# Reordering the stretch between dz and the dx loop of a fused transformer-block backward kernel: both dz halves together, dWq blocks between dKV and WK2, x normalised early, ring transposes ahead of those of WV2

## The chip, the cores and the metric

The kernel runs on one core of one Trainium2 chip. The metric is the device time of one execution in microseconds (us). The span of a profiled execution, from its first instruction to its last, is some 2 us shorter than its own timed value; what lies in between is not in the record, so spans are compared with spans and times with times.

## The reference, cut to what matters

The forward pass is a linear-attention block behind a LayerNorm, then a SwiGLU block behind another; S = 2048, D = 640, 32 heads of 20. The kernel returns the output and six gradients.

```python
def _A_ref(x, wqkv, wo):
    q, k, v = ...                       # x @ wqkv, 32 heads
    pq, pk = phi(q), phi(k)             # elu-like feature map
    kv = einsum("bhsd,bhse->bhde", pk, v)
    z  = einsum("bhsd->bhd", pk)
    o  = einsum("bhqd,bhde->bhqe", pq, kv) / (einsum("bhqd,bhd->bhq", pq, z)[..., None] + 1e-6)
    return o @ wo
h  = x + _A_ref(_layernorm(x), wqkv, wo)
h2 = h + _B_ref(_layernorm(h), w_gate, w_up, w_down)   # SwiGLU
# returned: h2 and the gradients of x, wqkv, wo, w_gate, w_up, w_down
```

The stretch in question belongs to the backward pass of the attention block: `dz` is the gradient of z, `dKV` that of kv, `WK2` and `WV2` are two weight matrices folded from dKV (WV2 is WK2 transposed), `dWq` and `dWk` are column blocks of the gradient of wqkv, and the last loop makes `dk`, `dxn` and from it the gradient of x, tile by tile.

## The kernel before: the parts that matter

TensorE and ScalarE are ordered by the framework's scheduler here; VectorE and the queue of SyncE (SP), which issues all DMA transposes, keep the order of the program. There are four PSUM tiles, the memory that matmuls write to, shared by everything (`mm`): a group of matmuls can take a tile only after VectorE or ScalarE has read out (evicted; "cast" where ScalarE makes bf16 of it) what an earlier group left there. The `ring` holds ten transposed operands for the coming tiles of the dx loop; a tile t is 128 of the 2048 rows. `dz` uses the TensorE array as tiles of 32 columns, all other matmuls here use all 128 columns; going from one to the other is called a tiling switch below.

```python
        ps_dz = mm("ps_dz")
        def dz_half(ci):                      # 16 matmuls on 32-column tiles of the array
            n0, n1 = NCH[ci]
            for t in range(ST):
                q = t % 4 * H
                nc.tensor.matmul(ps_dz[q:q + H, ci, :320], lhsT=nS1[:, t, :], rhs=pqs_tm[:, t, n0:n1], ...)
        dz_half(0)
        kv_blocks(dKVT, "ps_dkvt", ...)       # 6 blocks of 5 matmuls, each evicted by VectorE
        dz_half(1)
        ...                                   # dzE, dzL on VectorE out of ps_dz
        for t in range(ST):                   # x normalised, 16 tiles on VectorE
            nc.vector.tensor_scalar(out=xn_r[:, t, :], in0=xn_r[:, t, :], ...)
        def wk2(i):                           # 7 small matmuls, cast on ScalarE, transpose into WV2
            ps = mm("ps_wk2")
            mm_heads(ps, lambda j: wqkvT[:, 10 + j, i * P:(i + 1) * P], lambda j, a, b: dKVT[:, j, a:b])
            nc.scalar.copy(out=half(WK2[:, i, :]), in_=row(ps))
            nc.sync.dma_start_transpose(out=WV2[:, :, i * P:(i + 1) * P], in_=WK2[:, i, :])
        for i in range(DT):
            wk2(i)
        ps = mm("ps_dzb")                     # dz summed and broadcast: 4 matmuls of dzE, dzL
        ...
        for v in range(3):
            load_pqT(v)                       # 2 transposes each into the ring: pk, dq of tile v
        dwqk(0, 0, 3)                         # dWq blocks 0 to 2: 32 matmuls each, of x and dq
        for t in range(ST + LAG):             # the dx loop, LAG = 3
            ...                               # dk of tile t, transposed into the ring (SP)
            if t < HG: tr_cols(G[:, t, :], scr_GT, OH[t])             # one more transpose a tile (SP)
            elif t < 2 * HG: tr_cols(Y[:, t - HG, :], scr_Yt, OH[t - HG])
            u = t - LAG
            ...                               # dxn of tile u: dqT, pkT with WV2, dkT; 30 matmuls
            load_pqT(u + 3)
```

## Time and profile before

| | us |
|---|---|
| time, median of the first 3 runs | 821.05 (821.0 to 822.56) |
| span of the profiled execution | 820.0 |
| first dz matmul to first dk matmul, TensorE | 19.17 |
| first dk to first dxn matmul | 14.13 |
| first dxn matmul to the end | 169.7 |

From the profile's page, the busy time of the engines (us, share of the span, instructions), then the busy tenths of TensorE and its granted clock in 40 slices:

```profile
PE 813.3 (99%) x5540; PEld 521.0 (64%) x5540; DVE 442.9 (54%) x874; ACT 290.9 (35%) x412; POOL 187.6 (23%) x345
...
PE   8999999999999999999999999999999999999998
...
PEclk9999999999999999999999999999999999999999
```

TensorE is busy from end to end at full clock. Holes in it are short, and most of them do not show as idle time in the views: matmuls overlap in the trace (one of 320 columns lasts 299 ns there, while the next can start 136 ns after it). A hole is therefore read as the difference of two starts less the pace. The lines of the timelines of the stretch are in the prediction below.

### The profile page before, as it was taken

Reading aid. Unit: us, or ns where it says so; the run is one execution under the profiler, and the core shown is the slowest. Engines: PE = TensorE matmul, PEld = TensorE weight load, DVE = VectorE, ACT = ScalarE, POOL = GpSimd, SP = SyncE. Lnnn points to the kernel's source line nnn. Section 1 sums busy time; section 2 is a strip of 40 time slices with the busy share of each in tenths; the row PEclk is TensorE's granted clock in tenths of the full one; section 3 lists DMA queues with packets and bytes.
Section 4 is the critical chain, followed back from the end, with each engine's and each line's share of the span. In section 5 each row is a group of like instructions: output and inputs, shape, how many; then the busy total and the mean of one; then the engine's idle time right before and its main releaser. Section 6 shows DMA issues by size and latency. Waiting matters only on the chain.

```text
span 820.0 us, 14053 instructions
## 1 busy us (share of the span) xinstructions
PE 813.3 (99%) x5540; PEld 521.0 (64%) x5540; DVE 442.9 (54%) x874; ACT 290.9 (35%) x412; POOL 187.6 (23%) x345
## 2 busy tenths in 40 slices
PE   8999999999999999999999999999999999999998
PEld 6776656555555555555566677777776777777675
DVE  6878776891087018810760147787884366631212
ACT  6982422770184126500741122322322133322010
POOL 3330022322412412221125311211210111112330
PEclk9999999999999999999999999999999999999999
DMA  9994589998769997894498757976498999899962
GB/s 297 186 343 113 140 174 281 307 204 176 191 126 209 203 224 160 185 245 115 106 237 171 256 139 217 222 205 166 116 216 171 170 167 187 167 198 272 222 176 76
DMA packets 278321, 158.61 MB, mean 193 GB/s; under 512 B 235052, under 2 KB 264877, under 8 KB 278256
## 3 DMA queue, kind: packets, MB, share of 16 engines
q1 hardware_dynamic: 251696, 82.12, 54.3%
q0 software_dynamic: 17744, 64.45, 25.8%
q10 hardware_dynamic: 8816, 11.16, 4.3%
q8 instruction: 43, 0.70, 0.4%
q14 instruction: 22, 0.18, 0.1%
HBM read 47.68 MB, written 53.66 MB: 124 GB/s over the span
## 4 chain that ended last, share of the span: by engine, by line
PE 82%; DVE 9%; ACT 3%; DMA 3%; issue 1%; SPq 1%; ACTq 0%; POOL 0%; DVEq 0%
PE ps_dw L627 21%; PE ps_dhn L109 14%; PE ps_dxn L877 8%; PE ps_o L937 7%; PE ps_dwqk L109 5%; PE pu L563 5%; PE pg L558 5%; PE ps_y L109 3%; PE ps_gt L678 3%; PE ps_dp L109 3%; PE ps_dk L109 3%; PE pdm L385 2%; DMA xr<-in_A_x_dram 2%; PE ps_dm L385 2%; DVE st L134 1%
## 5 line engine op out<-in xcount | busy, mean ns | idle before, releaser
L109 PE MATMUL ps_dhn<-wgT,cols 128*128 128x320 bf16 x864 | 119.5, 299 | 0.0
L627 PE MATMUL ps_dw<-dd,hn 128*128 128x448 bf16 (+1 forms) x640 | 118.8, 346 | 0.0
L109 PEld LDWEIGHTS <-cols 128*128 128x128 bf16 x864 | 84.5, 98 | 32.9
L627 PEld LDWEIGHTS <-hn 128*128 128x128 bf16 x640 | 62.6, 98 | 54.2
L629 DVE CAST dwev<-ps_dw 128x896 bf16<-128x896 f32 (+3 forms) x12 | 10.9, 907 | 122.9 <-PE ps_dw L627 122.9
L629 ACT CAST dwev<-ps_dw 128x896 bf16<-128x896 f32 (+1 forms) x20 | 17.6, 879 | 160.5 <-PE ps_dw L627 139.9
L592 POOL DMA_DIRECT2D scr_dT<-stg x64 | 34.7, 542 | 168.9 <-DMA stg<-dd 168.2
L147 DVE CUSTOM_DVE_ANT_0 lb_a<-lb_dy,hn 128x640 bf16<-128x640 bf16 x32 | 26.4, 825 | 75.4 <-ACT lb_dy L145 75.4
L563 PE MATMUL pu<-wgu,hnT 128*128 128x448 bf16 (+1 forms) x320 | 63.6, 346 | 0.0
L558 PE MATMUL pg<-wgu,hnT 128*128 128x448 bf16 (+1 forms) x320 | 63.6, 346 | 0.0
L937 PE MATMUL ps_o<-wd,mT 128*128 128x320 bf16 (+3 forms) x462 | 61.3, 295 | 0.0
L627 PE MATMUL ps_dw<-m_s,dh 128*128 128x448 bf16 (+1 forms) x320 | 60.5, 346 | 0.1
L877 PEld LDWEIGHTS <-ring 128*128 128x128 bf16 x480 | 47.0, 98 | 18.2
L937 PEld LDWEIGHTS <-mT 128*128 128x128 bf16 (+1 forms) x462 | 41.8, 97 | 17.6 <-issue 2.6
L877 PE MATMUL ps_dxn<-wqkvT,ring 128*128 128x320 bf16 x320 | 51.3, 299 | 0.0
L627 PEld LDWEIGHTS <-dh 128*128 128x128 bf16 x320 | 31.3, 98 | 27.4 <-issue 0.4
L563 PEld LDWEIGHTS <-hnT 128*128 128x128 bf16 x320 | 31.3, 98 | 27.1
L558 PEld LDWEIGHTS <-hnT 128*128 128x128 bf16 x320 | 31.3, 98 | 27.0
L298 PE MATMUL ps_kq<-wqk,xnT 128*128 128x320 bf16 x320 | 46.4, 299 | 1.0 <-ACT xnT L290 1.0
L385 PEld LDWEIGHTS <-dh2T 128*128 128x128 bf16 x320 | 31.1, 98 | 25.1 <-issue 0.2
L385 PE MATMUL ps_dm<-wdT,dh2T 128*128 128x448 bf16 (+1 forms) x240 | 46.9, 344 | 0.1
L145 ACT ACTIVATE lb_dy<-ps_dhn,rstd 128x640 bf16<-128x640 f32 x16 | 12.7, 793 | 85.5 <-PE ps_dhn L109 85.5
(162 smaller groups left out, 1277.1 us busy)
## 6 DMA issues: line engine op xcount, KB each, us to landing
scr_dT<-stg POOLq DMA_DIRECT2D x48, 224.0 KB, 3.3
cols<-scr_dT POOLq DMA_DIRECT2D x6, 1728.0 KB, 8.0
scr_m<-m_s POOLq DMA_DIRECT2D x12, 448.0 KB, 4.7
cols<-scr_dT ACTq DMA_DIRECT2D x2, 1728.0 KB, 9.5
out_dram<-dwev POOLq DMA_DIRECT2D x30, 112.0 KB, 3.4
scr_dT<-stg POOLq DMA_DIRECT2D x16, 192.0 KB, 2.6
scr_pk<-pk SPq DMA_DIRECT2D x4, 640.0 KB, 8.4
scr_pq<-pqa SPq DMA_DIRECT2D x4, 640.0 KB, 8.7
```

Source lines behind the costliest of these rows:

```text
L109: nc.tensor.matmul(ps[:, ci, :320], lhsT=lhs(k), rhs=rhs(k, *NCH[ci]), start=(start and k == 0), stop=(stop and k == n - 1))
L147: nc.vector.tensor_tensor_reduce(out=a[:], in0=dy[:], in1=xhat, scale=1.0, scalar=0.0, op0=ALU.mult, op1=ALU.add, accum_out=sums[:, 1:2])
L298: nc.tensor.matmul(ps[:, ci, :320], lhsT=xnT[:, t, k, :], rhs=wqk[:, k, w0 + n0:w0 + n1], start=(k == 0), stop=(k == DT - 1))
L385: nc.tensor.matmul(ps[:, c, :w], lhsT=dh2T[:, kt, (t + c) * P:(t + c + 1) * P], rhs=wdT[:, kt, o:o + w], start=(kt == 0), stop=(kt == DT - 1))
L558: nc.tensor.matmul(pg[:, c, :w], lhsT=hnT[:, kt, (t + c) * P:(t + c + 1) * P], rhs=wg[:, kt, 0:w], start=(kt == 0), stop=(kt == DT - 1))
L563: nc.tensor.matmul(pu[:, c, :w], lhsT=hnT[:, kt, (t + c) * P:(t + c + 1) * P], rhs=wg[:, kt, w:2 * w], start=(kt == 0), stop=(kt == DT - 1))
L592: nc.gpsimd.dma_start(out=scr_dT[t + c, :, KO[g]:KO[g] + GK[g], :], in_=stg[:, :GK[g], :])
L627: nc.tensor.matmul(ps[:, c, :w], lhsT=lhs(t), rhs=rhs(t), start=(t == 0), stop=(t == ST - 1))
L629: copy(out=ev[:, :len(parts), :w], in_=ps[:, :len(parts), :w])
L678: nc.tensor.matmul(ps[:, ci, :320], lhsT=dh1[:, t, i * P:(i + 1) * P], rhs=pqs_tm[:, t, n0:n1], start=(t == 0), stop=(t == ST - 1))
L877: nc.tensor.matmul(ps[:, ci, :320], lhsT=lhs[:, i, :], rhs=rhs[:, i, n0:n1], start=(k == 0 and i == 0), stop=(k == 2 and i == DT - 1))
L937: nc.tensor.matmul(po(t, ci), lhsT=mTs[t // 4][r, t % 4, j, :], rhs=wd[r, j, n0:n1], start=(t, ci) not in opened, stop=last)
```

## The change

The intent is to take the waits out of TensorE between dz and the dx loop. The same instructions run in another order: the dz halves stand together, the dWq blocks are spread between dKV and the WK2 blocks so that there is work while ScalarE casts, the 16 normalisations that dWq needs are moved to where VectorE idled, and the first six transposes of the dx loop go ahead of those of WV2, which now come later.

```diff
+        for v in range(3):
+            load_pqT(v)
+        for t in range(ST):                   # x normalised: moved up
+            nc.vector.tensor_scalar(out=xn_r[:, t, :], ...)
         ps_dz = mm("ps_dz")
-        dz_half(0)
-        kv_blocks(dKVT, "ps_dkvt", ...)
-        dz_half(1)
+        for ci, (n0, n1) in enumerate(NCH):   # both halves
+            for t in range(ST): ...
+        kv_blocks(dKVT, "ps_dkvt", ...)
         ...                                   # dzE, dzL
-        for t in range(ST):
-            nc.vector.tensor_scalar(out=xn_r[:, t, :], ...)
-        for i in range(DT):
-            wk2(i)
+        dwqk(0, 0)
+        for i in range(3):
+            wk2(i)
+        dwqk(0, 1)
+        for i in range(3, DT):
+            wk2(i)
         ps = mm("ps_dzb")
         ...
-        for v in range(3):
-            load_pqT(v)
-        dwqk(0, 0, 3)
+        dwqk(0, 2)
         ...                                   # cut: the same calls with another signature
```

More of the change, by code (lines that the diff above doesn't have):

```diff
@@ L778 @@
         nc.vector.memset(dKVT, 0.0)
-        ps_dz = mm("ps_dz")
-        def dz_half(ci):
-            n0, n1 = NCH[ci]
-            for t in range(ST):
-                q = t % 4 * H
-                nc.tensor.matmul(ps_dz[q:q + H, ci, :320], lhsT=nS1[:, t, :], rhs=pqs_tm[:, t, n0:n1],
-                                 start=(t < 4), stop=(t >= ST - 4))
-        dz_half(0)
-        kv_blocks(dKVT, "ps_dkvt", lambda i, a, b: woT[:, i, a:b], lambda i, a, b: GT[:, i, a:b])
-        dz_half(1)
-        dzE = [wk("dzE"), wk("dzL")]
-        ps = ps_dz
-        nc.vector.tensor_tensor(out=half(dzE[0][:]), in0=row(ps), in1=half(E[:]), op=ALU.mult)
-        nc.vector.tensor_tensor(out=half(dzE[1][:]), in0=row(ps), in1=half(dzE[0][:]), op=ALU.subtract)
-        nc.vector.tensor_tensor(out=dzE[1][:], in0=dzE[1][:], in1=E[:], op=ALU.mult)
-        for t in range(ST):
-            nc.vector.tensor_scalar(out=xn_r[:, t, :], in0=xn_r[:, t, :], scalar1=mv1[:, t, 0:1],
-                                    scalar2=rstd1[:, t:t + 1], op0=ALU.subtract, op1=ALU.mult)
         wvk = strips.tile([P, 2, DT, D], BF16, name="wvk", tag="S")
@@ L802, with load_pqT @@
         WK2 = wvk[:, 1]
+        ring = strips.tile([P, 10, DT, P], BF16, name="ring", tag="S")
+        def load_pqT(v):
+            nc.sync.dma_start_transpose(out=ring[:, 4 + v % 3], in_=scr_pk[v * P:(v + 1) * P, :])
+            nc.sync.dma_start_transpose(out=ring[:, 7 + v % 3], in_=dq[v // 8][:, v % 8, :])
         def wk2(i):
@@ L808, in wk2, with dwqk @@
             nc.sync.dma_start_transpose(out=WV2[:, :, i * P:(i + 1) * P], in_=WK2[:, i, :])
-        for i in range(DT):
+        def dwqk(which, i):
+            ev = wk("dwqk", pool=i % 2)
+            ps = mm("ps_dwqk")
+            mm_row(ps, lambda t: xn_r[:, t, i * P:(i + 1) * P],
+                   lambda t, n0, n1: dq[t // 8][:, t % 8, n0:n1] if which == 0 else dk[:, t, n0:n1], ST)
+            nc.scalar.copy(out=half(ev[:]), in_=row(ps))
+            nc.gpsimd.dma_start(out=out_2[i * P:(i + 1) * P, which * D:(which + 1) * D], in_=ev[:])
+        for v in range(3):
+            load_pqT(v)
+        for t in range(ST):
+            nc.vector.tensor_scalar(out=xn_r[:, t, :], in0=xn_r[:, t, :], scalar1=mv1[:, t, 0:1],
+                                    scalar2=rstd1[:, t:t + 1], op0=ALU.subtract, op1=ALU.mult)
+        ps_dz = mm("ps_dz")
+        for ci, (n0, n1) in enumerate(NCH):
+            for t in range(ST):
+                q = t % 4 * H
+                nc.tensor.matmul(ps_dz[q:q + H, ci, :320], lhsT=nS1[:, t, :], rhs=pqs_tm[:, t, n0:n1],
+                                 start=(t < 4), stop=(t >= ST - 4))
+        kv_blocks(dKVT, "ps_dkvt", lambda i, a, b: woT[:, i, a:b], lambda i, a, b: GT[:, i, a:b])
+        dzE = [wk("dzE"), wk("dzL")]
+        nc.vector.tensor_tensor(out=half(dzE[0][:]), in0=row(ps_dz), in1=half(E[:]), op=ALU.mult)
+        nc.vector.tensor_tensor(out=half(dzE[1][:]), in0=row(ps_dz), in1=half(dzE[0][:]), op=ALU.subtract)
+        nc.vector.tensor_tensor(out=dzE[1][:], in0=dzE[1][:], in1=E[:], op=ALU.mult)
+        dwqk(0, 0)
[3 more added lines that the diff above has]
+        for i in range(3, DT):
             wk2(i)
@@ L814 @@
         nc.scalar.copy(out=half(dzb[:]), in_=row(ps))
-        def dwqk(which, i0=0, i1=DT):
-            for i in range(i0, i1):
-                ev = wk("dwqk", pool=i % 2)
-                ps = mm("ps_dwqk")
-                mm_row(ps, lambda t: xn_r[:, t, i * P:(i + 1) * P],
-                       lambda t, n0, n1: dq[t // 8][:, t % 8, n0:n1] if which == 0 else dk[:, t, n0:n1], ST)
-                nc.scalar.copy(out=half(ev[:]), in_=row(ps))
-                nc.gpsimd.dma_start(out=out_2[i * P:(i + 1) * P, which * D:(which + 1) * D], in_=ev[:])
-        ring = strips.tile([P, 10, DT, P], BF16, name="ring", tag="S")
-        def load_pqT(v):
-            nc.sync.dma_start_transpose(out=ring[:, 4 + v % 3], in_=scr_pk[v * P:(v + 1) * P, :])
-            nc.sync.dma_start_transpose(out=ring[:, 7 + v % 3], in_=dq[v // 8][:, v % 8, :])
-        for v in range(3):
-            load_pqT(v)
-        dwqk(0, 0, 3)
+        dwqk(0, 2)
         dk = big.tile([P, ST, D], BF16, name="dk", tag="B")
@@ L844 @@
             if t in (2, 3):
-                dwqk(0, t + 1, t + 2)
+                dwqk(0, t + 1)
             if t < ST:
@@ L870 @@
             if t >= ST:
-                dwqk(1, t - ST, t - ST + 1)
+                dwqk(1, t - ST)
             pkT, dqT, dkT = ring[:, 4 + u % 3], ring[:, 7 + u % 3], ring[:, u % 4]
@@ L890 @@
         nc.sync.dma_start(out=wd[64:, 13, :], in_=B_w_down[13 * P:F, :])
-        dwqk(1, LAG)
+        for i in range(LAG, DT):
+            dwqk(1, i)
         def dwo(j):
```

## The prediction

> **What bounds the kernel now.** I read the page first. Its first table gives TensorE 99% of the span and its second shows the granted clock at full speed in every slice, so the kernel is a single stream of matmuls with hardly a hole in it. A change that only reorders work can win nothing but the small holes that are left. The reordering of each engine's instructions by the change (counted in the built program, not timed) shows the same matmuls, casts, VectorE operations and transfers before and after: 0 added, 0 removed. So I looked for holes in the stretch that is reordered, from the two dz halves to the first dxn tile, in the timeline of TensorE:
>
> ```profile
> 616.93 0.73 PE L786 MATMUL ps_dz<-pqs_tm,nS 128*32 128x320 bf16 x16
> 617.59 1.61 PE L484 MATMUL ps_dkvt<-mats 128*128 128x120 bf16 x30
> 619.14 0.73 PE L786 MATMUL ps_dz<-pqs_tm,nS 128*32 128x320 bf16 x16
> 619.80 1.06 PE L128 MATMUL ps_wk<-mats,wqkvT 128*128 128x120 bf16 x21
> 621.06 1.05 PE L128 MATMUL ps_wk<-mats,wqkvT 128*128 128x120 bf16 x14 [0.20 <-ACT wvk L807]
> 621.95 0.30 PE L109 MATMUL ps_dzb<-dzE,ones 128*128 128x320 bf16 x1
> 622.18 0.30 PE L109 MATMUL ps_dzb<-dzL,ones 128*128 128x320 bf16 x1
> ...
> 622.58 13.68 PE L109 MATMUL ps_dwqk<-dq,hn 128*128 128x320 bf16 x96
> 636.10 2.88 PE L109 MATMUL ps_dk<-wvk,xnT_r 128*128 128x320 bf16 x20
> 638.82 4.51 PE L109 MATMUL ps_dwqk<-dq,hn 128*128 128x320 bf16 x32
> 643.16 1.52 PE L109 MATMUL ps_dk<-wvk,xnT_r 128*128 128x320 bf16 x10
> ```
>
> Columns: start, length, engine, line, operation, operands, count, and in brackets the idle time ahead. The starts carry the argument: lengths include the pipeline's tail, so the pace is the difference of starts. From the first dz matmul to the first dk matmul it is 636.10 - 616.93 = 19.17 us. The undisturbed pace of a 320-column matmul is read from the later dwqk block: (643.16 - 638.82)/32 = 0.1356 us.
>
> VectorE in the same stretch, from its timeline:
>
> ```profile
> 611.05 0.82 DVE L734 TENSOR_TENSOR dq<-dp,rall 128x640 bf16<-128x640 bf16 x1
> 618.07 1.45 DVE L486 TENSOR_TENSOR mats<-ps_dkvt,mask 128x120 bf16<-128x120 f32 x6 [6.19 <-PE ps_dkvt L484]
> 619.91 0.82 DVE L794 TENSOR_TENSOR dzE<-ps_dz,E 128x640 bf16<-128x640 f32 x1 [0.40 <-PE ps_dz L786]
> ...
> 621.63 0.49 DVE L796 TENSOR_TENSOR dzL<-dzL,E 128x640 bf16<-128x640 bf16 x1
> 622.04 5.79 DVE L798 TENSOR_SCALAR hn<-hn,mv,rstd 128x640 bf16<-128x640 bf16 x16
> ```
>
> It idles 6.19 us, then has to normalise 16 tiles of x just when the dwqk matmuls already want them. And the queue that issues the transposes:
>
> ```profile
> 616.06 15.18 SPq L660 DMA_TRANSPOSE wqkvT<-in_A_wqkv_dram  x10
> 631.34 7.75 SPq L808 DMA_TRANSPOSE wvk<-wvk  x5
> 639.26 1.20 SPq L828 DMA_TRANSPOSE ring<-scr_pk  x1
> ...
> 645.88 1.49 SPq L829 DMA_TRANSPOSE ring<-dq  x1
> 647.46 1.22 SPq L857 DMA_TRANSPOSE ring<-dk  x1
> ```
>
> One transpose follows another without a hole, 1.2 to 1.5 us each; the queue is full here although no engine waits for it yet.
>
> **What the Trainium skill says.** "TensorEngine Tiling (Array Packing)", Key Properties: changing the tiling mode drains TensorE. The trace agrees: dz uses 32-column tiles, and its 16 matmuls per half (four at a time, 4 steps of 0.136 = 0.54 us) take 617.59 - 616.93 = 0.66 us to the next group, so a switch back costs about 0.1 us; single starts show 0.08 to 0.10 us beyond the pace at each of four switches. "Perfetto Trace Analysis", Matmuls: independent groups should rotate through PSUM banks so that the evacuation of one overlaps the next group's matmuls. The trace agrees and shows the limit: a WK2 block is 7 matmuls or about 0.3 us, its cast on ScalarE 0.62 us (5 in 3.08), and with four PSUM tiles the fourth block waits. The same page, "DMA Instruction — HWDGE": what a profile shows of such a transfer is the making of its descriptors, not the data movement. The trace agrees: the issue of the first dk transpose lasts 1.22 us, while the view of transfers has it 3.6 us from issue to landing. The same page, "What DMA-bound means": a sequencer track that is solid DMA slices is itself the limit. That is the state of the transpose queue here.
>
> **The change part by part, on TensorE.**
> 1. Both dz halves together: four tiling switches become two. Saved: two of about 0.09, 0.18 us. Cost: none.
> 2. dWq blocks between dKV and WK2: now 32 dwqk matmuls (4.34 us) stand ahead of WK2 blocks 0 to 2, 32 more ahead of blocks 3 and 4. Before, the WK2 matmuls took 621.95 - 619.80 = 2.15 us. Unhindered, blocks 0 to 2 run 21 matmuls in 0.90 us (starts inside the first row), 0.043 each, so 35 need 1.51 us. Saved: 0.64 us, the two waits for ScalarE's casts. (The bracket shows only 0.20 because the tail of a matmul counts as busy.) What may come back: dwqk block 1 reuses the PSUM tile of block 0 (I looked at the addresses in the built program). Its cast ends about 0.89 us after the block (0.20 until it starts, 0.69 long), and three WK2 blocks lie between, 0.90 us. So a wait of 0 to 0.1 us; I put 0.05. The wait of dwqk block 0 for the fourth dKV eviction ties in the same way: about 0.
> 3. dzb after all of this: its second matmul waited for dzL, 622.18 - 621.95 = 0.23 against 0.136. Saved 0.09 us, for dzL will be ready some 8 us ahead.
> 4. x normalised ahead of dz: 96 dwqk matmuls took 636.10 - 622.58 = 13.52 us against 96 x 0.1356 = 13.02. Saved 0.50 us, the waits for the 16 normalisations. On VectorE those go into the idle 6.19 us: VectorE's earlier chain ended at 611.87, plus 16 x 0.362 = 5.79 gives 617.66. The order puts two of them ahead of the last nS (608.92 becomes about 609.7, needed at 616.93: harmless). The dKV evictions come after them: dkvt starts at 616.93 + 1.20 = 618.13 and its first eviction can start 0.48 later, at 618.61. So VectorE is free 0.9 us in time.
> Sum: 0.18 + 0.64 + 0.09 + 0.50 - 0.05 = 1.36 us. So the first dk matmul should start at 636.10 - 1.36 = 634.74, and the first dxn tile at 650.23 - 1.36 = 648.87, if nothing else holds it.
>
> 5. Ring transposes ahead of those of WV2. Here I expect most of the gain to be given back. In the queue there are 16 wqkvT transposes, then 5 + 6 others, then that of dk tile 0. The change swaps the five with the six; the dk transpose stays the twelfth after wqkvT, and the queue is already solid, so it is still issued at about 647.46 and lands at 647.46 + 3.57 = 651.03. Its operand is free much earlier (dk tile 0 is written at about 638 after the change). The dxn tile takes its three factors in the order dq, pk with WV2, dk; the dk part stands 10 matmuls in, at 651.58 before, a margin of 0.55 us. After the change TensorE wants it at 648.87 + 1.36 = 650.23. So it waits 651.03 - 650.23 = 0.80 us. The swap itself moves nothing on that path. Nor does it harm: the third WV2 transpose, needed for the first half of the columns at 649.55, takes the place of the third of the ring (landed 645.94) or a little later, and the fifth, needed at 651.6, that of the last (landed 650.19).
> Net: 1.36 - 0.80 = 0.56 us. Later tiles have margins of their own that I worked out from issues and landings: the closest is the dq transpose of tile 4, landed 0.70 us ahead of its use; 0.56 us of lead still fits, barely. After tile 12 the margins are above 6 us, and the end (dW_k blocks, output rows) follows TensorE, so what is left at tile 4 should reach the end.
>
> **The rivals.**
> A. No new wait: the queue gets to dk earlier. For it: the last of the 11 issues took between 1.2 and 2.0 us, some of it back-pressure of the DMA engines, and dwqk's stores come earlier. Then all 1.36 us stays: 819.7. Against it: the number of transposes ahead is the same and 1.2 us each is their floor.
> B. The dk transpose lands later. Landing takes 2.6 to 5.8 us in this ring, so another microsecond is possible; then the wait is 1.8 and the change ends at -0.4, 821.5 us.
> C. The dxn loop becomes bound by the queue: it issues four transposes a tile, about 5.3 us, against 5.43 us of matmuls. A lead of TensorE is then eaten at tiles 4 to 8, whose margins were 0.7 to 1.4. It makes 820.5 to 821.0.
> D. VectorE late with the 16 normalisations (if the reload of x came late). It landed at about 602, so I give this little; it would cost up to 1 us.
>
> **Range and chances.** 821.05 - 0.56 gives 820.5. A at 819.7 and B or C at 821 to 821.5 set the range 819.5 to 821.5; the three runs before spread over 821.0 to 822.56, so part of it is noise. Nothing here comes near 2%, which is 16 us: both outer chances are 0.01.
>
> **What would show it right or wrong.** In the timeline after: dz as one row of 32 and dkvt at about 618.1; no bracket ahead of WK2; three dwqk rows of 32, each 4.34 us from start to start; dk at about 634.7. Then, new: a wait of TensorE for the ring of about 0.8 us inside the first dxn tile, with the dk transpose still issued near 647.5. If dk starts near 634.7 and the span is shorter by the whole 1.4, step 5 was wrong; if dk starts after 635.3, steps 2 or 4 were. If there are waits for the ring at tiles 4 to 8, it was C.

## The result, and the profile after

| | before | after |
|---|---|---|
| median time of the runs by then | 821.8 us (4 runs, 821.0 to 822.96) | 820.66 us (4 runs, 819.94 to 822.01) |
| ratio | | 0.9987, 95% interval 0.9967 to 1.0007 |
| the same later, 9 and 5 runs | 821.93 us | 820.72 us, ratio 0.9987, interval 0.9974 to 0.9999 |
| span of the profiled execution | 820.0 us | 819.0 us |
| first dz to first dk matmul | 19.17 us | 17.97 us |
| first dk to first dxn matmul | 14.13 us | 14.13 us |

A ratio is the mean time of one kernel's fast runs over that of the other's in the same rounds, so it is not quite the ratio of the medians. The change is worth about a microsecond, at the edge of what the timing can tell, and the trace says where it comes from. The timeline of TensorE after the change:

```profile
617.18 1.27 PE L811 MATMUL ps_dz<-pqs_tm,nS 128*32 128x320 bf16 x32
618.38 1.62 PE L484 MATMUL ps_dkvt<-mats 128*128 128x120 bf16 x30
619.99 4.51 PE L109 MATMUL ps_dwqk<-dq,hn 128*128 128x320 bf16 x32
624.33 1.05 PE L128 MATMUL ps_wk<-mats,wqkvT 128*128 128x120 bf16 x21
625.32 4.51 PE L109 MATMUL ps_dwqk<-dq,hn 128*128 128x320 bf16 x32
629.66 0.75 PE L128 MATMUL ps_wk<-mats,wqkvT 128*128 128x120 bf16 x14
630.26 0.30 PE L109 MATMUL ps_dzb<-dzE,ones 128*128 128x320 bf16 x1
630.39 0.30 PE L109 MATMUL ps_dzb<-dzL,ones 128*128 128x320 bf16 x1
...
635.14 2.88 PE L109 MATMUL ps_dk<-wvk,xnT_r 128*128 128x320 bf16 x20
```

Every dWq block takes 4.34 us from start to start (624.33 - 619.99), the undisturbed pace; the bracket ahead of the WK2 blocks is gone; the second dzb matmul follows the first after 0.13 us. VectorE has moved its 16 normalisations into its idle time (six stand one by one further up, ten in this row), and still idles ahead of the dKV evictions:

```profile
613.44 3.65 DVE L805 TENSOR_SCALAR hn<-hn,mv,rstd 128x640 bf16<-128x640 bf16 x10
618.85 1.45 DVE L486 TENSOR_TENSOR mats<-ps_dkvt,mask 128x120 bf16<-128x120 f32 x6 [1.76 <-PE ps_dkvt L484]
```

And the queue of the transposes:

```profile
614.42 15.08 SPq L660 DMA_TRANSPOSE wqkvT<-in_A_wqkv_dram  x10
629.54 1.28 SPq L785 DMA_TRANSPOSE ring<-scr_pk  x1
...
638.43 6.81 SPq L792 DMA_TRANSPOSE wvk<-wvk  x5
645.33 1.23 SPq L851 DMA_TRANSPOSE ring<-dk  x1
```

The swap is there: the ring first, then WV2 (`wvk`). But the transpose of dk tile 0 is issued at 645.33 and not at 647.46. It landed at 649.09, 1.54 us ahead of its use, and TensorE did not wait in the first dxn tile. That is the step of the prediction that the first trace contradicts outright, and the experiments had to say why.

### The profile page after: what moved, and what is told of

Read it like the earlier page. It is cut to its first block, busy times and chain, and to the rows that moved or that the text cites. A ratio compares the mean times of both kernels' runs of the same rounds, so it can differ in the third digit from the quotient of the medians.

```text
span 819.0 us, 14057 instructions
## 1 busy us (share of the span) xinstructions
PE 812.0 (99%) x5540; PEld 521.7 (64%) x5540; DVE 442.4 (54%) x874; ACT 291.0 (36%) x412; POOL 188.2 (23%) x345
## 4 chain that ended last, share of the span: by engine, by line
PE 92%; DVE 4%; ACT 2%; DMA 1%; issue 1%; POOL 0%; DVEq 0%; ACTq 0%
PE ps_dw L627 21%; PE ps_dhn L109 14%; PE ps_dxn L871 8%; PE ps_o L932 7%; PE pu L563 7%; PE pg L558 7%; PE ps_dwqk L109 5%; PE ps_dm L385 5%; PE ps_y L109 3%; PE ps_dp L109 3%; PE ps_dk L109 3%; PE ps_gt L678 3%; PE ps_a L109 3%; PE pdm L385 2%; DVE st L134 1%; ACT phi_e L307 1%
```

## The experiments

**Theory.** On TensorE's path the change is worth what its four parts take from the distance between the first dz and the first dk matmul. The transposes have no part in it: their order does not matter, and the queue is near its limit, but its phase against TensorE differs from run to run, and the first profile of before had caught it late. **Rivals.** The swap of the transposes is what kept the first dxn tile from waiting; the change itself moved the queue earlier; or the queue has slack after all. The expectations below count the parts of the change: 1 is dz, 2 dWq among WK2, 3 the early x (step 4 of the prediction), 4 the ring transposes (its step 5).

All results in one table. "dz to dk" is from the first dz to the first dk matmul. "Ten" is the start of the ten wqkvT transposes, "ahead of dz" how long that is before the first dz matmul, "dk after" the issue of the dk transpose of tile 0 counted from there, "dk ahead" how long before its first use it landed. "Least dq" is the smallest margin of a dq transpose in the dx loop, with the tile. "Tail" is from the first dxn matmul to the end. All in us; the clock was at full speed in these stretches but for two runs named below.

| profile | dz to dk | ten | ahead of dz | dk after | dk ahead | least dq (tile) | tail |
|---|---|---|---|---|---|---|---|
| before | 19.17 | 616.06 | 0.87 | 31.40 | 0.55 | 0.70 (4) | 169.74 |
| e5, before again | 19.17 | 615.93 | 1.46 | 30.44 | 1.56 | 0.80 (10) | 169.74 |
| after | 17.97 | 614.42 | 2.76 | 30.91 | 1.54 | 0.76 (9) | 169.76 |
| e6, after again | 17.97 | 614.14 | 3.81 | 30.34 | 3.08 | 2.48 (4) | 169.75 |
| e11, after once more | 17.97 | 615.02 | 1.64 | 30.19 | 1.06 | 0.05 (11), waits | 169.97 |
| e1, dz split | 18.03 | 613.34 | 4.29 | 30.32 | 2.91 | 1.66 (11) | 169.74 |
| e2, x late | 22.35 | 612.53 | 4.30 | 29.82 | 7.54 | 0.28 (11) | 169.74 |
| e3, dWq late | 18.84 | 615.24 | 4.49 | 30.67 | 4.53 | 2.69 (4) | 169.75 |
| e4, ring late | 17.97 | 615.35 | 3.25 | 30.72 | 1.66 | 0.94 (9) | 169.76 |
| e7, three more transposes | 17.97 | 616.39 | 1.44 | 34.93 | waits | 2.71 (4) | 175.79 |
| e8, no small waits | 17.72 | 615.01 | 1.17 | 30.64 | 1.07 | 0.04 (11), waits | 170.98 |
| e10, the same again | 17.72 | 613.09 | 4.07 | 30.54 | 3.20 | 1.62 (11) | 169.74 |
| e9, queue relieved too | 17.72 | 613.85 | 3.98 | 30.57 | 2.83 | 2.22 (4) | 169.74 |

The table also tells how sharp the instrument is: three profiles of one kernel give the same dz to dk, and the tail repeats to 0.02 us where nothing waits. The scatter of the total times lies elsewhere: the first dz matmul starts anywhere from 616.2 to 619.7 us. Some 2 us of that range are there by 67 us (the first `ps_dm` matmul starts at 66.7 to 68.7), the rest comes mostly from waits between 100 and 140 us, as large as 1.65 us in one profile, all in a part that no kernel here touches. Nor does the change cost anything just ahead of dz, where VectorE now has its normalisations: from the first `ps_gt` matmul to the first dz matmul are 23.18 us in all thirteen profiles.

### e1: the dz halves split again

```diff
-        for ci, (n0, n1) in enumerate(NCH): ...   # both halves
+        dz_half(0)
         kv_blocks(dKVT, "ps_dkvt", ...)
+        dz_half(1)
```

> Undoes part 1 alone: the second dz half goes back behind dKV, so there are four tiling switches again. Measure: from the first dz matmul to the first dk matmul on TensorE; 17.96 us in the changed kernel, 19.17 before. Theory: the two extra switches cost 0.18 us, but a dz half between dKV and the first dWq block hides the 0.14 us that the first dWq matmul now loses (0.169 us after the last dKV matmul where 0.025 is the pace), because its PSUM tile is still being evicted by VectorE. So 18.00, and the first dWq matmul without that loss. Rival (the merge is worth its switches, and the 0.14 has another cause): 18.14.

Measured: 18.03 us, the theory's value (18.00) and not the rival's (18.14). Correct result; one run at 821.57 us beside one of before at 822.35. TensorE:

```profile
617.63 0.73 PE L812 MATMUL ps_dz<-pqs_tm,nS 128*32 128x320 bf16 x16
618.29 1.61 PE L484 MATMUL ps_dkvt<-mats 128*128 128x120 bf16 x30
619.84 0.73 PE L812 MATMUL ps_dz<-pqs_tm,nS 128*32 128x320 bf16 x16
```

From dkvt to what follows are 619.84 - 618.29 = 1.55 us here, where the changed kernel has 619.99 - 618.38 = 1.61, and the last of the thirty starts show the difference: 0.11 us to the dz half against 0.17 us to the dWq block where the pace is 0.03. In the changed kernel the first dWq matmul waits 0.14 us for a PSUM tile that VectorE is still evicting; with a dz half in between that wait is covered, and the two extra tiling switches (0.08 and 0.10 us) cost a little more than that. So keeping the dz halves together is worth 0.06 us and not 0.18: a wait took the place of most of what was removed.

### e2: x normalised late again

```diff
-        for t in range(ST): nc.vector.tensor_scalar(out=xn_r[:, t, :], ...)   # ahead of dz
         ...
         nc.vector.tensor_tensor(out=dzE[1][:], in0=dzE[1][:], in1=E[:], op=ALU.mult)
+        for t in range(ST): nc.vector.tensor_scalar(out=xn_r[:, t, :], ...)
```

> Undoes part 3 alone: the 16 normalisations of x stand behind the dz eviction on VectorE again, the dWq blocks stay early. Theory: dWq needs the normalised x at once; VectorE is done with the dz chain only some 2.5 us after dKV and then makes a tile each 0.36 us. TensorE waits some 2.7 us and then follows at VectorE's pace for a while: first dz to first dk 20.5 to 21.5 us, worse than before (19.17). Rival (the scheduler orders TensorE around it, and the early normalisation is worth only the 0.5 us that was lost before): at most 18.5.

Measured: 22.35 us, the rival is out, and it is worse than the theory's 20.5 to 21.5. Correct; one run at 825.0 us. The timeline of TensorE, then the view by stretches (stretch, length, busy us of PE, PEld, DVE, ACT, POOL, granted clock, DMA share, GB/s):

```profile
618.03 1.62 PE L484 MATMUL ps_dkvt<-mats 128*128 128x120 bf16 x30
622.48 0.31 PE L109 MATMUL ps_dwqk<-dq,hn 128*128 128x320 bf16 x1 [2.83 <-DVE hn L816]
```

```profile
620.00:623.00 3.00, 0.52 (x7) 0.43 (x8) 2.93 (x6) 0.00 (x0) 0.00 (x0) 0.99 1.04 352
623.00:626.50 3.50, 3.50 (x28) 2.52 (x26) 3.50 (x11) 2.08 (x3) 0.00 (x0) 0.52 1.24 132
```

The wait for the first normalised tile is 2.83 us, as expected (2.7). What the theory missed is the second row: behind the wait TensorE ran 3.5 us at a granted clock of 0.52, and 0.48 x 3.5 makes an estimated 1.7 us more. So "x early" is what makes dWq ahead of WK2 possible at all: without it the same reordering is 3.2 us slower than the kernel before. It also has a gain of its own, the 0.50 us of waits that the dWq blocks had before; e3, with x early and dWq late, has it too (from its first dWq matmul to the first dk matmul, 99 matmuls, are 13.45 us, 0.136 each).

### e3: the dWq blocks behind WK2 again

```diff
-        dwqk(0, 0)
-        for i in range(3): wk2(i)
-        dwqk(0, 1)
-        for i in range(3, DT): wk2(i)
+        for i in range(DT): wk2(i)
         ...                                   # dzb
-        dwqk(0, 2)
+        for i in range(3): dwqk(0, i)
```

> Undoes part 2 alone: all five WK2 blocks and dzb stand ahead of the three dWq blocks; dz together and x early stay. Theory: the waits of WK2 blocks 3 and 4 for ScalarE's casts return (0.65 us), WK2 directly behind dKV also waits some 0.2 us for the last dKV evictions, and the two small waits of the changed kernel (0.14 and 0.09) vanish: 17.96 + 0.65 + 0.2 - 0.23 = about 18.6 us from first dz to first dk. Rival (the gain comes from the early x and the merged dz alone): 17.9 or less.

Measured: 18.84 us, where the theory had about 18.6 and the rival 17.9 or less. Correct; one run at 824.26 us, in which the stretch ahead of dz was the slowest of all profiles (dz at 619.73), so its total says nothing. TensorE:

```profile
622.54 1.09 PE L128 MATMUL ps_wk<-mats,wqkvT 128*128 128x120 bf16 x21
623.93 1.05 PE L128 MATMUL ps_wk<-mats,wqkvT 128*128 128x120 bf16 x14 [0.31 <-ACT wvk L791]
```

The waits for ScalarE's casts are back (0.46 and 0.30 us beyond the pace), with 0.14 us ahead of the first WK2 block, where the last dKV evictions are waited for, and 0.17 us among the dzb matmuls, which the theory had left out: the scheduler puts two dWq matmuls there, and the first of them starts as the cast of the third WK2 block ends (625.08). The place of the dWq blocks is the largest single part: 18.84 - 17.97 = 0.87 us.

### e4: the ring transposes behind those of WV2 again

```diff
-        for v in range(3):
-            load_pqT(v)                       # ahead of WK2
         ...                                   # WK2, dzb
+        for v in range(3):
+            load_pqT(v)
         dwqk(0, 2)
```

> Undoes part 4 alone: the six ring transposes stand behind the five of WV2 again. Theory: the queue is solid and holds the same eleven transposes ahead of that of dk tile 0, so the issue of the latter stands 30.5 to 32 us after the start of the ten wqkvT transposes as in both kernels (31.4 before, 30.9 after), and first dz to first dk stays 17.96 us, no wait in the first dxn tile unless the ten transposes themselves start late. Rival (the swap is what kept the first dxn tile from waiting): a wait of TensorE for the ring in the first dxn tile, with the dk or dq transpose of it landing after its use.

Measured: dz to dk 17.97 us, the dk transpose issued 30.72 us after the ten begin, landed 1.66 us ahead of its use, no wait. Correct; one run at 822.46 us. The queue:

```profile
615.35 14.95 SPq L660 DMA_TRANSPOSE wqkvT<-in_A_wqkv_dram  x10
630.39 7.58 SPq L792 DMA_TRANSPOSE wvk<-wvk  x5
...
646.07 1.51 SPq L851 DMA_TRANSPOSE ring<-dk  x1
```

The swap is worth nothing here. It takes margin from WV2 (the third of its transposes landed 5.5 us ahead of its use in the changed kernel, 15.4 here) and gives it to the ring (the dq transpose of tile 0: 14.6 us and 7.5). Both have plenty, and dk tile 0, which has the least of the three, keeps its place.

### e5, e6 and e11: both kernels again, for the phase of the queue

No edit.

> The kernel before once more, for its trace. What is asked: is the start of the ten wqkvT transposes a property of the kernel or of the run? It was 616.06 us in the profile of before, but 614.42, 613.34, 612.53, 615.24 and 615.35 in five kernels that do the same work up to there. Theory (it varies by the run, for it follows 6 transposes that the loads of xnT and x hold back): anywhere from 612 to 617 here, and the dk transpose of tile 0 issued 30 to 31.5 us after it; so the margin of that transpose ahead of its use, 0.55 us in the first profile, is between 0 and 4 us. First dz to first dk 19.16 us again, to 0.05. Rival (the change made the queue earlier): 616 again, margin 0.5 again.

> The changed kernel once more, for its trace and its time. Theory: first dz to first dk 17.97 us to 0.05, first dxn to the end 169.76 us to 0.05, all scatter of the total lies ahead of dz; so the true gain is 1.19 us and the ratio of the times 0.9985, inside the interval if that is narrow enough. Rival (part of the lead is lost later in some runs, at the ring): dxn to the end longer than 170, ratio nearer to 1.

> The changed kernel beside the relieved one in the same rounds, for the times. Theory: first dz to first dk 17.97 us, first dxn to the end 169.75 us; total 1.1 to 1.3 us less than before, and 0.1 to 0.3 us more than the relieved kernel, which the timing can hardly tell. Rival: a wait in the loop that eats the lead.

Measured: the kernel before gives dz to dk 19.17 us once more, and its dk transpose is 1.56 us ahead of its use instead of 0.55. The queue's ten begin at 615.93, near the first profile, so e5 alone does not part the two views on that point. e7, which has the changed kernel's whole order up to there, has the latest start of all, 616.39. What decides, though, is the start against TensorE: the ten begin 0.87 and 1.46 us ahead of dz in the two profiles of before, and 1.17 (e8) to 4.49 us (e3) ahead in the eleven with a changed order. The ranges overlap, with e8 and e7 (1.44) as late as e5, so the change does not force an earlier queue; but both profiles of before lie at the late end, and that the change moves the queue on average is not excluded by two of them. Over the thirteen profiles the ten begin anywhere from 612.5 to 616.4, and the dk transpose follows 29.8 to 31.4 us later where eleven transposes stand between. The first profile of before was the second latest in the one and the latest in the other; five of its 21 issues took over 1.6 us, three in each other profile with 21. The changed kernel has 1.54, 3.08 and 1.06 us in three profiles: a wait in the first dxn tile did not occur.

In e11 a part of the lead was lost later: the dq transpose of tile 11 landed as TensorE came to it, and the tail is 169.97, longer by 0.22 us. The times: e6 820.88 us (6 runs) against 821.88, ratio 0.9979, interval 0.9951 to 1.0007 (among the eleven runs of before is one of 828.96 us at a granted clock of 0.995, without a trace; leaving it out, the means stand at 0.9988); e11 820.72 us (5 runs) against 821.93, ratio 0.9987, interval 0.9974 to 0.9999. From the traces the expected ratio is 1 - 1.20/821.9 = 0.9985.

### e7: three needless transposes in the queue

```diff
         for v in range(3):
             load_pqT(v)
+        for v in range(3):                    # into ring places not in use yet
+            nc.sync.dma_start_transpose(out=ring[:, 3 - v], in_=scr_pk[v * P:(v + 1) * P, :])
```

> The changed kernel with three needless transposes (of pk, into ring places that are not in use yet) ahead of those of WV2, some 1.3 us each. Theory: the queue is solid, so each pushes the dk transpose of tile 0 back by its issue: issued 34 to 36 us after the ten wqkvT transposes begin, landing 0.5 to 3.5 us after TensorE wants it, and TensorE waits that long in the first dxn tile; the end comes later by the same. That is the wait that the prediction expected, made on purpose. Rival (the queue has slack, holes swallow the three): dk transpose still some 31 us after the ten begin, no wait.

Measured: the dk transpose is issued 34.93 us after the ten begin, as the theory had it, and TensorE waits. Correct; one run at 827.69 us. TensorE, and the stretch behind the wait:

```profile
650.60 0.84 PE L873 MATMUL ps_dxn<-wvk,ring 128*128 128x320 bf16 x5
655.36 2.57 PE L873 MATMUL ps_dxn<-wqkvT,ring 128*128 128x320 bf16 x10 [3.92 <-DMA ring<-dk]
```

```profile
655.30:659.00 3.70, 3.64 (x15) 2.13 (x16) 0.00 (x0) 0.00 (x0) 0.00 (x0) 0.55 1.00 113
```

The wait is 3.92 us, a little over the 3.5 that had been given; the queue was also late in this run, with the ten only 1.44 us ahead of dz. So the queue has no slack: the three issues took 4.1 us with the pauses between them, the dk transpose is issued 4.4 us later than in the mean of the changed kernel's three profiles, and the wait that the prediction described is real where the queue is late enough. Again the matmuls after the hole ran at about half the clock, 0.55 over 3.7 us, and the tail is longer by 6.0 us, not by 4.

### e8 and e10: without the two small waits

```diff
-        kv_blocks(dKVT, "ps_dkvt", ...)
+        for j0 in range(0, HG, 2):            # two dKV blocks share a PSUM tile, evicted after both
+            ps = mm("ps_dkvt")
+            for j in (j0, j0 + 1): ...        # matmuls into ps[:, j % 2]
+            for j in (j0, j0 + 1): ...        # VectorE out of ps[:, j % 2]
         ...                                   # below: calls drawn together on one line each
-        dwqk(0, 0); wk2(0); wk2(1); wk2(2); dwqk(0, 1); wk2(3); wk2(4); dzb; dwqk(0, 2)
+        dwqk(0, 0); wk2(0); wk2(1); dwqk(0, 1); wk2(2); wk2(3); dwqk(0, 2); wk2(4); dzb
```

> The changed kernel without the two small waits it left: two dKV blocks share a PSUM tile, so the first dWq block takes a tile that was evicted earlier; and only two WK2 blocks stand between dWq blocks, so the second dWq block takes the tile of dz and not the one whose cast ScalarE has just begun. Order: dWq 0, WK2 0 and 1, dWq 1, WK2 2 and 3, dWq 2, WK2 4, dzb. Theory: 0.14 and 0.10 us fall away, first dz to first dk 17.73 us; total 0.24 us less than the changed kernel, too little for the timing to tell. Rival (one wait is replaced by another, say of dzb or of the first dk matmuls for the last casts): 17.9 or more.

> The kernel without the two small waits once more, unchanged, for its trace. Theory (the wait of 1.21 us at tile 11 was the run's: the smallest margin of the dq transposes in the loop has been 0.04 to 2.7 us in ten profiles, whatever the kernel): first dz to first dk 17.72 us, and first dxn to the end 169.75 us, or a wait at another of tiles 9 to 11. Rival (it belongs to the kernel): again a wait of about 1.2 us at tile 11.

Measured: 17.72 us in both, so the two small waits (0.14 and 0.10) are understood and gone. Of these, 0.15 came back directly behind, in the first dk tile, where the fifth matmul now waits for the cast of the last WK2 block; up to the first dxn matmul 0.09 us is left. Correct; e8 820.95 us (6 runs) against 821.88, ratio 0.9979, interval 0.9953 to 1.0004, e10 one run at 820.88. In the first of the two profiles the dx loop waited; the view of waits of e8:

```profile
PE ps_dxn L882 <- DMA ring<-dq: 1.0, 1, 1.0
```

That is tile 11, and it cost 1.21 us from start to start. In the second profile of the same kernel there is no such wait. So it is not in every run of the kernel, and e11 shows a small one at the same tile in the changed kernel.

### e9: the queue relieved as well

```diff
-            elif t < 2 * HG:
-                tr_cols(Y[:, t - HG, :], scr_Yt, OH[t - HG])
-            if t == 2 * HG:
+            elif HG + 3 <= t < 2 * HG + 3:    # no Y transpose at tiles 6 to 8
+                tr_cols(Y[:, t - HG - 3, :], scr_Yt, OH[t - HG - 3])
+            if t == 2 * HG + 3:
```

> The kernel without the two small waits, and with the queue relieved: the six transposes of Y are issued at tiles 9 to 14 of the dxn loop and not at 6 to 11, that of KV at 15; all other engines have the same instructions in the same order. In tiles 6 to 8 the queue then has three transposes a tile (some 4.0 us) against 5.43 us of matmuls. Theory (the 1.21 us that the kernel without the small waits lost at tile 11 was the queue, which lives on the edge with four a tile): the margins of the dq transposes at tiles 9 to 12 grow to 3 us or more, no wait in the loop, first dxn to the end 169.75 us. Rival (the wait has to do with the reordering and not with the queue): it returns at tile 11.

Measured: the dq margins at tiles 9 to 12 are 3.9 to 4.3 us in this profile, and the tail is 169.74; the smallest margin in the loop is 2.22 us, at tile 4, ahead of the relief. Correct; 820.65 us (5 runs) against 821.93, ratio 0.9988, interval 0.9974 to 1.0001. The unrelieved kernels have 0.04 to 4.4 us at tiles 9 to 11, and two of their profiles (e6, e7) were as good by themselves, so one profile speaks for the relief but does not prove it. In time this kernel cannot be told from the changed one beside it (820.65 and 820.72): its 0.09 us on TensorE's path, and the 0.2 to 1.2 us that it might save in some runs, are under what five rounds resolve.

## Why the prediction was right or wrong

**The bound and the kind of change: right.** TensorE stayed at 99%, nothing was added, and the only thing won was holes between matmuls that hardly show as idle time.

**Step 1, the tiling switches: right in its size, wrong in what it bought.** The two switches do cost 0.08 and 0.10 us (e1). But the tie at the fourth dKV eviction, put at about 0, was a wait of 0.14 us, and it is only open because the dz half no longer stands there. Net 0.06 us and not 0.18.

**Step 2, WK2: right.** The two waits are gone; the wait for the cast of dWq block 0 came out at 0.10 us where the prediction had 0.05.

**Steps 3 and 4, dzb and x: right.** 0.13 us from dzb to dzb, 4.34 us for each dWq block, VectorE free 1.76 us ahead of the first eviction (0.9 had been worked out, for the normalisations interleave with other operations better than their sum). e2 shows that step 4 is a condition of step 2.

**The sum of the four: 1.20 us measured, 1.36 predicted.** The missing 0.16 is the 0.14 of the eviction and the 0.05 more of the cast, to the rounding. By group, as differences of starts in the two timelines (to 0.01 us):

| group of matmuls | before | after | gain | predicted |
|---|---|---|---|---|
| dz, 32 | 1.32 | 1.20 | 0.12 | 0.18, with the next row |
| dKV, 30 (with the wait or switch behind it) | 1.55 | 1.61 | -0.06 | |
| WK2, 35 | 2.15 | 1.59 | 0.56 | 0.64 - 0.05 |
| dzb, 4 | 0.63 | 0.54 | 0.09 | 0.09 |
| dWq, 96 | 13.52 | 13.02 | 0.50 | 0.50 |

**Step 5, the queue: wrong.** The step that failed reads "so it is still issued at about 647.46". The reasoning ahead of it holds: the swap moves nothing (e4), the dk transpose keeps its place, the queue has no slack (e7: three more transposes, a wait of 3.92 us). What fails is the time of day. The prediction took an issue time from one profile, to be compared with a use in another run, and gave a wait of 0.80 us. In the first profile of the changed kernel the transpose was issued 2.13 us earlier than that (645.33): 1.64 us because the ten began earlier, 0.49 because the issues behind them took less. It landed 1.94 us earlier and TensorE came 0.95 us earlier, so the margin grew from 0.55 to 1.54 us. The queue's ten begin within a range of 3.9 us from run to run and the rest adds 1.6 us; the profile it used was late in both. In three profiles of the changed kernel the transpose landed 1.06 to 3.08 us ahead of its use, with the lead of 1.20 already taken. Had the queue stood as in the first profile of before, the wait would have been an estimated 1.20 - 0.55 = 0.65 us, and as in the second, none: the mechanism is real, its occurrence was not shown in any profile of this kernel.

**Rival A, the queue gets to dk earlier: right.** It looked to the shorter issues, which gave the smaller part (0.49 of 2.13 us). The prediction's "1.2 to 1.5 us each" holds for the ring lines it shows; the merged rows of ten and of five hold single issues of up to 2.2 us. That back-pressure makes the long ones is not shown, though the DMA engines were busier during them (mean share 1.12 over the 42 of more than 1.6 us in the thirteen traces, 0.87 over the others).

**Rival C, the loop bound by the queue: partly right.** In one of three profiles of the changed kernel 0.22 us of the lead went at tile 11, not at tiles 4 to 8; in one of two of e8, 1.21 us.

**The number.** 820.5 us was predicted, 820.66 measured. That is luck: two errors offset each other. The gain is 1.1 us by the times and 1.2 by the trace, twice the 0.56 that was forecast; and the 821.05 it was taken from, a median of three runs, was low: with more runs before is at 821.8 to 821.9.

**What stays open.** What sets the start of the ten wqkvT transposes was not tried; that the loads of xnT and x ahead of them hold the queue back was only argued. The traces go with it: all loads are issued at the same distance from dz in all thirteen, but the last of xnT lands 2.6 us (before) to 8.1 us (e10) ahead of dz, and the ten begin in almost the same order, 0.87 to 4.49 us ahead. Which of the two holds back the other, and whether the change has a part in it, stays open. Nor was it tried what makes TensorE late ahead of 67 us and wait between 100 and 140 us, which is larger than the gain, nor what happened in the run of before at 828.96 us.

## What to carry to other kernels

Where one engine is busy 99% of the time, read starts and not lengths: the waits taken away here were up to 0.36 us each and only one showed as idle time in the views. Before moving a piece away, ask what it was covering: the dz half covered an eviction, and a dWq block placed without its normalised x in time costs more than the whole change wins. And a margin between two queues that run freely against each other is not a number from one profile; take several, because 0.55 us in one profile of the kernel before was 1.56 in the next, and 1.06 to 3.08 in three of the changed one.

## What the Trainium skill lacked or had wrong

- "TensorEngine Tiling (Array Packing)", Key Properties: says that a change of tiling mode drains TensorE, but gives no cost. Here a switch between 128-column and 32-column tiles costs 0.08 to 0.10 us, in every profile.
- "TensorE: Matmul & The Clock Gate", What's actually happening: puts the fall to half the clock behind an idle window of about 3.4 us. Here a hole of 2.83 us (e2; 3.01 from start to start) was enough, followed by 3.5 us at a granted clock of 0.52; a hole of 3.92 us (e7) by 3.7 us at 0.55. In both the clock's own records have 3.41 us at 0.50, beginning 0.47 and 0.33 us after the first matmul behind the hole. A hole of 1.8 us from start to start (e6, at 136 us) was followed by full clock, 1.00. The page's two speeds agree with the traces.
- "Perfetto Trace Analysis", Optimization Strategy: tells to look for gaps between slices. On TensorE the recorded length of a matmul hides part of a hole: 0.36 us lost between starts was 0.20 us idle, and 0.30 us (the next one) 0.14, which the timeline and the view of waits leave out. The pace has to be subtracted from the difference of starts. The page warns elsewhere that matmul busy time is a bad metric because matmuls are pipelined, but does not carry that over to the gaps.
- No page gives the time that the sequencer of this chip needs to issue a DMA transpose of a 128 x 640 tile ("DMA: Bandwidth & Descriptors" has only AWS's cycle counts for other sizes, without a measurement). It was 1.2 to 1.3 us here unhindered, up to 8.0 us when held back (e11), and four a tile nearly fill a loop of 5.43 us.
